# Linear attention and gated feed-forward: small PE products regrouped by array shape, accumulators moved between bank pools

## Chip, cores, metric

One core of one Trainium2 chip. The metric is the device time of one execution in microseconds (us). Of the core's engines, PE (TensorE) does the matrix products, DVE (VectorE), ACT (ScalarE) and POOL (GpSimd) the rest, and SP (SyncE) issues transfers. Matrix products are written to accumulators in PSUM, a memory that the kernel divides into banks.

## The reference, cut to what matters

```python
for b in range(nb):                                   # blocks of 64 tokens, state carried along
    intra = einsum('bhic,bhjc->bhij', qb, kb) * Dmask # scores, masked with decay
    intra = einsum('bhij,bhjd->bhid', intra, vb)
    inter = einsum('bhid,bhde->bhie', qb * lam_pow, kv_state)
    out[:, :, sl] = intra + inter
    kv_state = lam_block * kv_state + einsum('bhsd,bhse->bhde', kb_dec, vb)
# x: [3072 tokens, 512]
y = (sigmoid(x @ w_gate) * (x @ w_val)) @ w_out       # 512 -> 1536 -> 512
```

Batch 4 ("b" below), 8 heads of 64, 768 tokens. The kernel goes through the tokens in six steps of 128 (step 0 to 5). In each it makes for every b and head a score block, masks it on the DVE, multiplies it with v (masked products) and adds q times state (state products); then it renews the state (sums). The dense products of one step run between the attention work of the next.

## The kernel before

`ps_at` has five PSUM banks for attention, `ps_ff` three for the dense products.

```python
ps_at = ctx.enter_context(tc.tile_pool(name="ps_at", bufs=5, space=bass.MemoryType.PSUM))
ps_ff = ctx.enter_context(tc.tile_pool(name="ps_ff", bufs=3, space=bass.MemoryType.PSUM))
...
def piece_s(n, bs, pool=ps_at, tag="ps"):             # scores: 64 rows x 128 columns of the array
    for b in bs:
        bp, i = b // 2, b % 2
        sp = [pool.tile([128, HP, C], FP32, name=f"sp{u}", tag=tag) for u in range(2)]
        for hp in range(HP):
            for u in range(2):
                us = slice(u * 64, (u + 1) * 64)
                nc.tensor.matmul(sp[u][:, hp, :], lhsT=KS[n, bp][us, hp // 2, i, hp % 2, :],
                                 rhs=QS[n, bp][us, hp // 2, i, hp % 2, :], ...)
...
def piece_a(n, pairs):
    OP = {...ps_at.tile(...)...}
    for ...:                                          # state products: 64 x 64
        nc.tensor.matmul(OP[bp, u][half(e), x, i, :], lhsT=Sb[half(u), 2 * bp + i, 2 * e + x, :],
                         rhs=QS[n, bp][half(u), e, i, x, :], ...)
    for ...:                                          # masked products: 128 x 64
        intra(n, 2 * bp + i, OP[bp, u][:, x, i, :], 2 * x + u, False, i == 1 and x == 1)
    ...                                               # ACT copies OP into XT
...
def c(n, *pairs):                                     # sums: 128 x 64
    for bp in pairs:
        pool, tag = (ps_at, "ps") if bp == 0 or n == 0 else (ps_ff, "ff")
...
for n in range(2, NSTEP):                             # nx = n + 1
    ...
    gv(n, 10)                                         # dense: gate and value of one tile
    sc(nx, 0); gv(n, 11); m(nx, 0)                    # scores of b 0, 1; masks
    piece_po(n, 0)                                    # dense: output of one b
    sc(nx, 1); m(nx, 1)                               # scores of b 2, 3
    piece_po(n, 1); piece_po(n, 2)
    a(nx, 0, 1); c(nx, 0, 1)                          # state and masked products, sums
    piece_po(n, 3)
```

## Time and profile before

| | before |
|---|---|
| time, median of six runs | 226.31 us (226.23 to 227.33) |
| span from first to last instruction, profiled run | 224.2 us |
| PE busy | 97% of the span |
| DVE, ACT, POOL busy | 47%, 35%, 35% |
| matmuls | 1744 |

A PE row of the timeline has start, duration, line, operation, operands, the array's rows*columns, the shape, and the count of merged matmuls. The duration includes a modelled end and overlaps the next row, so read the difference of two starts. The operands are named gp (gate), vp (value) and po (output) for the dense products, sp for scores, op for state and masked products, cp for sums. An array shape of 64*128 means that two matmuls run side by side, 64*64 four, 128*64 two.

### The profile page before, as it was taken

What the parts mean: (1) busy time and instruction counts of PE and PEld (TensorE: products, weight loads), DVE (VectorE), ACT (ScalarE), POOL (GpSimd) and SP (SyncE); (2) the same over time, 40 slices, a digit from 0 to 9 for tenths busy, and PEclk for the clock granted to TensorE, in tenths of its full rate; (3) what the DMA queues carried; (4) which work ended last, traced back from release to release, by engine and by line L of the source; (5) the groups of instructions that cost most, each with busy time, mean ns of one, the idle gap of its engine ahead of it and who ended that gap; (6) DMA issues with size and microseconds to landing.
All of it is one profiled execution on the core that took longest, in us unless ns stands there. A gap on an engine that the chain in (4) does not pass through costs nothing.

```text
span 224.2 us, 4261 instructions
## 1 busy us (share of the span) xinstructions
PE 217.6 (97%) x1744; PEld 114.3 (51%) x1744; DVE 105.9 (47%) x193; ACT 79.5 (35%) x151; POOL 79.2 (35%) x78
## 2 busy tenths in 40 slices
PE   7789999999999999999999999999999999999994
PEld 2454455888854454444455444446444445444443
DVE  7797758585411713336722445642335840333300
ACT  5664343435422234333225333115333225333221
POOL 8998687983592008920006940000000000000000
PEclk9999999999999999999999999999999999999999
DMA  6999999999999993999021999021930012100022
GB/s 110 155 171 191 191 176 155 164 177 170 157 163 163 226 225 106 202 158 100 1 96 67 218 144 136 0 96 47 169 69 0 0 57 86 47 3 0 0 94 95
DMA packets 106419, 25.70 MB, mean 115 GB/s; under 512 B 97056, under 2 KB 103456, under 8 KB 106400
## 3 DMA queue, kind: packets, MB, share of 16 engines
q0 software_dynamic: 81792, 13.90, 80.4%
q1 hardware_dynamic: 23568, 11.28, 21.2%
q10 hardware_dynamic: 1040, 0.26, 0.5%
q8 instruction: 13, 0.21, 0.4%
q14 instruction: 6, 0.05, 0.1%
HBM read 28.32 MB, written 6.29 MB: 154 GB/s over the span
## 4 chain that ended last, share of the span: by engine, by line
PE 92%; DMA 3%; POOL 3%; issue 0%; ACT 0%; DVE 0%; POOLq 0%
PE po L476 27%; PE gp L413 21%; PE vp L419 20%; PE gp L427 6%; PE gp L448 5%; PE vp L454 5%; DMA vb<-in_v_dram 3%; PE op L306 3%; PE sp L293 2%; PE op L318 1%; PE po L465 1%; POOL kb L91 1%; PE cp L397 1%; POOL qb L91 1%; POOL vb L91 1%
## 5 line engine op out<-in xcount | busy, mean ns | idle before, releaser
L422 DVE TENSOR_TENSOR ht<-sg,vp 128x512 bf16<-128x512 bf16 x53 | 36.5, 688 | 62.6 <-PE vp L419 62.5
L476 PE MATMUL po<-WO,ht 128*128 128x512 bf16 x276 | 61.9, 379 | 0.0
L413 PE MATMUL gp<-XT,WG 128*128 128x512 bf16 x212 | 54.4, 379 | 0.0
L419 PE MATMUL vp<-XT,WV 128*128 128x512 bf16 x212 | 54.4, 379 | 0.0
L416 ACT ACTIVATE sg<-gp 128x512 bf16<-128x512 f32 x53 | 31.6, 597 | 59.3 <-PE gp L413 59.3
L476 PEld LDWEIGHTS <-ht 128*128 128x128 bf16 x276 | 26.3, 98 | 31.0
L419 PEld LDWEIGHTS <-WV 128*128 128x128 bf16 x212 | 20.7, 98 | 25.0
L413 PEld LDWEIGHTS <-WG 128*128 128x128 bf16 x212 | 20.4, 98 | 24.5
L479 ACT COPY ob<-po 128x512 f32<-128x512 f32 x23 | 13.5, 586 | 52.2 <-PE po L476 50.4
L204 DVE TENSOR_TENSOR MT<-sp,mask 128x512 bf16<-128x512 f32 x40 | 25.2, 683 | 8.7 <-PE sp L293 8.7
L375 POOL TENSOR_TENSOR sd<-Sb,dec 128x512 f32<-128x512 bf16 x8 | 8.2, 1042 | 40.6 <-DVE Sb L404 40.6
L448 PE MATMUL gp<-XT,WG 128*128 128x256 bf16 x96 | 14.4, 273 | 0.0
L454 PE MATMUL vp<-XT,WV 128*128 128x256 bf16 x96 | 14.4, 273 | 0.0
L458 DVE TENSOR_TENSOR ht<-sg,vp 128x256 bf16<-128x256 bf16 x24 | 10.0, 420 | 8.6 <-PE vp L454 8.6
L451 ACT ACTIVATE sg<-gp 128x256 bf16<-128x256 f32 x24 | 9.2, 384 | 13.0 <-PE gp L448 11.8
L366 POOL TENSOR_TENSOR kd<-kb,kds 128x1024 bf16<-128x1024 bf16 x6 | 11.3, 1906 | 5.0 <-DMA kb<-in_k_dram 5.0
L91 POOL DMA_DIRECT2D vb<-in_v_dram x10 | 12.7, 1279 | 0.7 <-DMA WG<-in_moe_w_gate_dram 0.6
L404 DVE TENSOR_TENSOR Sb<-cp,sd 128x512 bf16<-128x512 f32 x8 | 5.2, 686 | 15.5 <-PE cp L397 15.5
L333 ACT CAST XT<-op 128x512 bf16<-128x512 f32 x19 | 9.9, 598 | 2.1 <-PE op L306 2.0
L448 PEld LDWEIGHTS <-WG 128*128 128x128 bf16 x96 | 9.2, 98 | 1.7 <-issue 0.2
L454 PEld LDWEIGHTS <-WV 128*128 128x128 bf16 x96 | 9.4, 98 | 1.1
L77 POOL DMA_DIRECT2D qb<-in_q_dram x8 | 9.4, 1183 | 0.0
(80 smaller groups left out, 165.4 us busy)
## 6 DMA issues: line engine op xcount, KB each, us to landing
out_dram<-ob SPq DMA_DIRECT2D x21, 256.0 KB, 2.0
kb<-in_k_dram POOLq DMA_DIRECT2D x10, 256.0 KB, 8.5
qb<-in_q_dram POOLq DMA_DIRECT2D x8, 256.0 KB, 8.3
vb<-in_v_dram POOLq DMA_DIRECT2D x4, 512.0 KB, 13.9
WO<-in_moe_w_out_dram POOLq DMA_DIRECT2D x3, 512.0 KB, 8.7
WV<-in_moe_w_val_dram POOLq DMA_DIRECT2D x5, 256.0 KB, 8.7
WG<-in_moe_w_gate_dram POOLq DMA_DIRECT2D x4, 256.0 KB, 8.3
qb<-in_q_dram POOLq DMA_DIRECT2D x6, 128.0 KB, 9.0
```

The costliest lines, as they stand in the source:

```text
L91: nc.gpsimd.dma_start(out=lst[n][:, b0:b1], in_=src[b0:b1, :, sl, :].rearrange("b h s d -> s (b h) d"))
L204: nc.vector.tensor_tensor(out=out.rearrange("p (e x) c -> p e x c", e=2), in0=x.rearrange("p (e x) c -> p e x c", e=2), in1=mask.rearrange ...
L366: nc.gpsimd.tensor_tensor(out=KD[n][:, e], in0=K[n][:, e], in1=kds[:, e::2].unsqueeze(1).unsqueeze(3).to_broadcast([128, B, HP, D]), op=AL ...
L413: nc.tensor.matmul(gp, lhsT=WG[:, mt, fs], rhs=x[:, mt, :], start=(mt == 0), stop=(mt == NMT - 1))
L416: nc.scalar.activation(sg, gp, AF.Sigmoid)
L419: nc.tensor.matmul(vp, lhsT=WV[:, mt, fs], rhs=x[:, mt, :], start=(mt == 0), stop=(mt == NMT - 1))
L422: nc.vector.tensor_mul(HT[n, ft], sg, vp)
L427: nc.tensor.matmul(ps[:, lo:hi], lhsT=W[:, mt, ft * 128:(ft + 1) * 128], rhs=x[:, mt, lo:hi], start=(mt == 0), stop=(mt == NMT - 1))
L448: nc.tensor.matmul(gp[:, cs], lhsT=WG[:, mt, fs], rhs=x[:, mt, cs], start=(mt == 0), stop=(mt == NMT - 1))
L454: nc.tensor.matmul(vp[:, cs], lhsT=WV[:, mt, fs], rhs=x[:, mt, cs], start=(mt == 0), stop=(mt == NMT - 1))
L476: nc.tensor.matmul(po, lhsT=HT[n, ft][:, tt * 128:(tt + 1) * 128], rhs=WO[:, ft, :], start=(ft == 0), stop=(ft == NFT - 1))
L479: nc.scalar.copy(ob, po)
```

## The change

Its intent: fewer changes of array shape. The scores of the last b (in step 1, of every b) are cut in two halves of 64 columns, which gives them the 64x64 shape of the state products, and the state products move next to them. In steps 2 to 5 the scores of the other three b's share one visit of the PE. The second sum of each step and one dense accumulator (v11) move to the attention banks.

```diff
-    def piece_s(n, bs, pool=ps_at, tag="ps"):
+    def piece_s(n, bs, homes=("ps", "ps"), parts=1):
+        w = C // parts
...
-                    nc.tensor.matmul(sp[u][:, hp, :], lhsT=KS[n, bp][us, hp // 2, i, hp % 2, :],
+                    for z in range(parts):
+                        zs = slice(z * w, (z + 1) * w)
+                        nc.tensor.matmul(sp[u][zs, hp, :], lhsT=KS[n, bp][us, hp // 2, i, hp % 2, zs],
...
+    def piece_x(n, bp, homes=("ps", "ps")):           # the state products of the old piece_a
...
     def c(n, *pairs):
-            pool, tag = (ps_at, "ps") if bp == 0 or n == 0 else (ps_ff, "ff")
-            cp = pool.tile([128, 2, HP, D], FP32, name="cp", tag=tag)
+            cp = ps_at.tile([128, 2, HP, D], FP32, name="cp", tag="ps")
...
+    def most_scores(n):
+        piece_s(n, [0, 1])
+        piece_s(n, [2], ("ps", "ff"))
+        piece_m(n, 2, (1,))
+    def other_masks(n): ...
+    def last_scores(n):
+        piece_s(n, [3], parts=2)
+        piece_m(n, 3)
+        piece_x(n, 0)
+        piece_x(n, 1, ("ps", "ff"))
+    def rest(n):
+        piece_a(n, 0, 1)
+        if n + 1 < NSTEP:
+            c(n, 0, 1)
+    def pair(bp):                                     # step 1
+        piece_s(1, [2 * bp], ("ff", "ps"), parts=2)
+        piece_m(1, 2 * bp)
+        piece_s(1, [2 * bp + 1], parts=2)
+        piece_x(1, bp)
...
-    v11 = psum()
+    v11 = psum_at("ps").rearrange("p h c -> p (h c)")
...
-        sc(nx, 0)
+        most_scores(nx)
         gv(n, 11)
-        m(nx, 0)
+        other_masks(nx)
         piece_po(n, 0)
-        sc(nx, 1)
-        m(nx, 1)
         piece_po(n, 1)
+        last_scores(nx)
         piece_po(n, 2)
-        a(nx, 0, 1)
-        if nx + 1 < NSTEP:
-            c(nx, 0, 1)
+        rest(nx)
         piece_po(n, 3)
```

More of the change, by code (lines that the diff above doesn't have):

```diff
@@ L283, with psum_at @@
     SP = {}
-    def piece_s(n, bs, pool=ps_at, tag="ps"):
+    def psum_at(which):
+        pool, tag = (ps_ff, "ff") if which == "ff" else (ps_at, "ps")
+        return pool.tile([128, HP, C], FP32, name="sp", tag=tag)
+    def piece_s(n, bs, homes=("ps", "ps"), parts=1):
+        w = C // parts
         for b in bs:
             bp, i = b // 2, b % 2
-            sp = [pool.tile([128, HP, C], FP32, name=f"sp{u}", tag=tag) for u in range(2)]
+            sp = [psum_at(homes[u]) for u in range(2)]
             for hp in range(HP):
@@ L292, in piece_s @@
                     us = slice(u * 64, (u + 1) * 64)
-                    nc.tensor.matmul(sp[u][:, hp, :], lhsT=KS[n, bp][us, hp // 2, i, hp % 2, :],
-                                     rhs=QS[n, bp][us, hp // 2, i, hp % 2, :],
-                                     start=(hp == 0), stop=(hp == HP - 1), skip_group_check=True)
+                    for z in range(parts):
+                        zs = slice(z * w, (z + 1) * w)
+                        nc.tensor.matmul(sp[u][zs, hp, :], lhsT=KS[n, bp][us, hp // 2, i, hp % 2, zs],
+                                         rhs=QS[n, bp][us, hp // 2, i, hp % 2, :],
+                                         start=(hp == 0), stop=(hp == HP - 1), skip_group_check=True)
             SP[n, b] = sp
     def piece_m(n, b, us=(0, 1)):
-        if us[0] == 0:
+        if (n, b) not in MT:
             MT[n, b] = mtp.tile([128, 2, HP, C], BF16, tag="MT", name="MT")
@@ L308, in intra, with piece_a @@
                              start=start, stop=stop, skip_group_check=True)
-    def piece_a(n, pairs):
-        OP = {(bp, u): ps_at.tile([128, 2, 2, C], FP32, name="op", tag="ps")
-              for bp in pairs for u in range(2)}
-        for bp in pairs:
-            for i in range(2):
-                for x in range(2):
-                    for u in range(2):
-                        for e in range(2):
-                            nc.tensor.matmul(OP[bp, u][half(e), x, i, :],
-                                             lhsT=Sb[half(u), 2 * bp + i, 2 * e + x, :],
-                                             rhs=QS[n, bp][half(u), e, i, x, :],
-                                             start=(i == 0 and x == 0), stop=False,
-                                             skip_group_check=True)
+    OP = {}
+    def piece_x(n, bp, homes=("ps", "ps")):
+        for u in range(2):
+            pool, tag = (ps_ff, "ff") if homes[u] == "ff" else (ps_at, "ps")
+            OP[bp, u] = pool.tile([128, 2, 2, C], FP32, name="op", tag=tag)
+        for i in range(2):
+            for x in range(2):
+                for u in range(2):
+                    for e in range(2):
+                        nc.tensor.matmul(OP[bp, u][half(e), x, i, :],
+                                         lhsT=Sb[half(u), 2 * bp + i, 2 * e + x, :],
+                                         rhs=QS[n, bp][half(u), e, i, x, :],
+                                         start=(i == 0 and x == 0), stop=False,
+                                         skip_group_check=True)
+    def piece_a(n, *pairs):
         for bp in pairs:
@@ L332, in piece_a @@
                 cp = nc.vector.tensor_copy if n == 1 and bp == 0 and u else nc.scalar.copy
-                cp(XT[n][:, u::2, 2 * bp:2 * bp + 2, :], OP[bp, u])
+                cp(XT[n][:, u::2, 2 * bp:2 * bp + 2, :], OP.pop((bp, u)))
     def piece_a0(b, split=()):
@@ L511, in first @@
     def first():
-        piece_s(0, [2], ps_ff, "ff")
+        piece_s(0, [2], ("ff", "ff"))
         piece_m(0, 2, (0,))
@@ L544, in t, with other_masks @@
         piece_t(n, bp)
-    def sc(n, bp):
-        piece_s(n, [2 * bp, 2 * bp + 1])
-        piece_m(n, 2 * bp)
-    def m(n, bp):
-        piece_m(n, 2 * bp + 1)
-    def a(n, *pairs):
-        piece_a(n, pairs)
+    def most_scores(n):
+        piece_s(n, [0, 1])
+        piece_s(n, [2], ("ps", "ff"))
+        piece_m(n, 2, (1,))
+    def other_masks(n):
+        piece_m(n, 0)
+        piece_m(n, 1)
+        piece_m(n, 2, (0,))
+    def last_scores(n):
[12 more added lines that the diff above has]
+        piece_x(1, bp)
     def gv(n, *fts):
@@ L607 @@
     prod(0, 9, v9)
-    sc(1, 0)
-    m(1, 0)
+    pair(0)
+    piece_m(1, 1)
     gv(0, 10)
@@ L613 @@
     sigm(0, 11, g11)
-    a(1, 0)
-    v11 = psum()
+    piece_a(1, 0)
+    v11 = psum_at("ps").rearrange("p h c -> p (h c)")
     mm_part(v11, WV, 0, 11, 0, TCH)
@@ L623 @@
     gvh(1, 0, 6, 7)
-    sc(1, 1)
+    pair(1)
     gvh(1, 0, 8)
-    m(1, 1)
+    piece_m(1, 3)
     gvh(1, 0, 9, 10)
-    a(1, 1)
+    piece_a(1, 1)
     c(1, 0, 1)
@@ L640 @@
     piece_po(0, 3)
-    sc(2, 0)
-    m(2, 0)
+    most_scores(2)
+    other_masks(2)
     piece_po(1, 0)
-    sc(2, 1)
-    m(2, 1)
     piece_po(1, 1)
+    last_scores(2)
     piece_po(1, 2)
-    a(2, 0, 1)
-    c(2, 0, 1)
+    rest(2)
     piece_po(1, 3)
```

## The prediction

> **What bounds the kernel now.** I read the page's head first, then who waited for whom on the PE, then the PE in order of time, then the DVE and the DMA landings at the places where the PE is late.
>
> ```profile
> span 224.2 us, 4261 instructions
> PE 217.6 (97%) x1744; PEld 114.3 (51%) x1744; DVE 105.9 (47%) x193; ACT 79.5 (35%) x151; POOL 79.2 (35%) x78
> PE wm L153 <- DVE ip L119: 1.2, 1, 1.2
> PE tk L238 <- DMA kb<-in_k_dram: 0.5, 1, 0.5
> ```
>
> The PE is busy for 97% of the span at a granted clock of 1.000, every other engine for at most half, and the longest waits of the matmuls lie in the first microseconds. So the time is the PE's stream, and a change that leaves its matrix work alone can only win what stands between the matmuls. The busy column hides that: a matmul of 512 columns is given 379 ns, though in a run they start 216 ns apart. I therefore count from start to start. One step of the loop, PE in order of time (start us, us, engine line, operation, names, array rows*columns, shape, count):
>
> ```profile
> 104.91 1.03 PE L419 MATMUL vp<-XT,WV 128*128 128x512 bf16 x4
> 105.87 0.62 PE L293 MATMUL sp<-QS,KR 64*128 64x128 bf16 x16
> 106.42 1.04 PE L413 MATMUL gp<-XT,WG 128*128 128x512 bf16 x4
> ...
> 108.16 2.75 PE L476 MATMUL po<-WO,ht 128*128 128x512 bf16 x12
> 110.85 0.62 PE L293 MATMUL sp<-QS,KR 64*128 64x128 bf16 x16
> 111.40 5.35 PE L476 MATMUL po<-WO,ht 128*128 128x512 bf16 x24
> 116.68 0.64 PE L318 MATMUL op<-QS,Sb 64*64 64x128 bf16 x32
> 117.25 1.08 PE L306 MATMUL op<-MT,vb 128*64 128x128 bf16 x32
> 118.17 0.67 PE L397 MATMUL cp<-vb,kd 128*64 128x64 bf16 x32
> 118.78 2.76 PE L476 MATMUL po<-WO,ht 128*128 128x512 bf16 x12
> ```
>
> What to see: the four vp matmuls take 105.87 - 104.91 = 0.96 us, where four others take 0.86 (4 x 216 ns). The missing 0.10 us is spent whenever the array shape (the number pair) changes next. It is there again at 110.85 (2.69 for twelve, against 12 x 0.216 = 2.59), at 116.68 (5.28 against 5.18), after each group of scores, from 64*64 to 128*64, and from 128*64 back to 128*128. It is not there between op and cp at 118.17, which share 128*64: 0.92 for 16 pairs of 56 ns. The single records give the rest: in 64*128 two score matmuls start 3 to 4 ns apart and the next pair 56 ns after the last; in 64*64 four matmuls start 3 to 4 ns apart and the next four 56 ns later; the first step of a group adds 10 to 24 ns. So 16 scores are 8 x 56 + 10 + 0.10 us = 0.55, as shown, and 32 state products are 8 x 56 + 24 + 0.10 us = 0.57, as shown.
>
> **What the Trainium skill says.** "TensorEngine Tiling (Array Packing)", Key Properties: changing the tiling mode, not just the tile, drains the TensorE. The trace agrees: 0.10 us at each change of shape and none without. "TensorE: Matmul & The Clock Gate", Part 3: tiles of one mode run at the same time, about 4 ns apart; the trace has 3 to 4 ns. "Perfetto Trace Analysis", TensorE lifecycle: the reported end of a matmul is an estimate; the trace agrees (379 against 216 ns). The same page, Optimizing Tensor Performance: independent groups should rotate through PSUM banks so that evacuation overlaps the next group; two places below show what a short rotation costs here.
>
> **The change, part by part.**
> Changes of shape. In each of steps 2 to 5 the PE now leaves the dense products three times: for scores (in, out), for scores (in, out), and for state products, masked products and sums (in, 64*64 to 128*64, out). That is 7 changes. The new order on the PE, read from both built programs, is 24 scores in 64*128 (in, out), then after two output groups 16 half-width scores and 32 state products all in 64*64 (in, out), then after one more output group masked products and sums in 128*64 (in, out): 6 changes. Step 1 has for each of its two pairs of b 2 + 3 = 5 changes and gets 2 + 2 = 4, as both its score groups become 64*64 and stand with the state products. So 4 + 2 = 6 changes go, plus a few ns of group start: 6 x 0.105 = 0.63 us.
>
> Added matmuls. The halved scores make 8 extra matmuls and 8 extra weight loads for each b so treated: one in each of steps 2 to 5, four in step 1, so 64 in all (1744 becomes 1808). A b had 8 score matmuls in 4 pairs and gets 16 in 4 fours; a pair in 64*128 and a four in 64*64 both take 56 ns, so 4 x 56 = 224 ns before and after. So I put the cost at zero.
>
> Banks. Accumulators rotate: the dense products through three banks, attention through five, so a new one waits for the reader of the third (fifth) back. Two waits of the PE are of this kind, too short for the wait view because the estimated ends cover them (two PE lines, then the DVE line that ends the wait):
>
> ```profile
> 39.51 0.60 PE L454 MATMUL vp<-XT,WV 128*128 128x256 bf16 x4
> 40.08 0.60 PE L448 MATMUL gp<-XT,WG 128*128 128x256 bf16 x4
> 39.34 0.69 DVE L440 TENSOR_TENSOR ht<-sg,gp 128x512 bf16<-128x512 bf16 x1 [0.34 <-PE gp L427]
> ...
> 51.44 0.60 PE L454 MATMUL vp<-XT,WV 128*128 128x256 bf16 x4
> 52.07 0.60 PE L448 MATMUL gp<-XT,WG 128*128 128x256 bf16 x4
> 50.91 1.29 DVE L404 TENSOR_TENSOR Sb<-cp,sd 128x512 bf16<-128x512 f32 x2 [0.64 <-PE cp L397]
> ```
>
> Four 256-column matmuls take 0.437 us elsewhere. From 39.51 they take 0.57: the next gp wants the bank of v11, free at 39.34 + 0.69 = 40.03, and starts at 40.08, 0.14 late. From 51.44 they take 0.63: vp wants the third bank back, that of the second sum, which the DVE leaves at 50.91 + 1.29 = 52.20. This costs 0.20. In the new kernel v11 and that sum take attention banks; the third one back is then one that the ACT has read long before. Both waits should go: 0.34 us. In steps 2 to 4 the same kind of sum costs nothing today (the output group after it hides it).
>
> Sum: 0.63 + 0.34 = 0.97 us, all on the PE's path, out of 226.27: 225.3 us. The start-up (to 34 us) and the last step's dense work are untouched.
>
> **The rivals.**
> 1. New bank waits. Scores of three b's hold all five attention banks and one dense bank. A mask takes 0.60 us from start to start on the DVE. In step 3 the 24 scores would end near 106.8; the mask that frees the dense bank ends near 107.5, and its next user, an output group, starts near 108.4. The other five masks follow the last gate product (near 109.3) and end near 112.3; the first small matmul that needs one of their banks is at 113.7. So margins are 0.9 and 1.3 us. In step 1 they are thin: the masked products of the first pair would start near 37.5 with the last mask done near 37.3, and those of the second pair need the last mask about 0.3 us after it is done. A wait here would give back 0.1 to 0.3 us: 225.6.
> 2. The issue of small matmuls becomes the bound. 48 in a row in 64*64 at 14 ns each, instead of 32 (or 16 in step 1), with weight loads of 106 ns against 94 for the 64*128 ones. For: no run of this length is in the trace. Against: 32 + 32 + 32 small ones stand in a row at 116.68 with no slowing, the last 32 still at 16 ns each. If the halves cost double, 8 x 0.22 us would be lost: near 227.1.
> 3. A transfer takes the place of the wait. The first transposed K of step 2 lands at 72.14, and the scores start at 73.00; they would now come near 73.00 - 0.21 - 0.34 = 72.45. That leaves 0.3 us. Earlier output stores share the queues; if the landing slips, up to 0.3 us comes back. Later landings (95.4 for use at 105.9) are far away.
> 4. Nothing at all for the bank waits, if the DVE's queue is simply as late for the next user: the new owner of each bank is one read by the ACT or earlier by the DVE, so I think it unlikely; it would make 225.6.
>
> **Range and chances.** The 0.63 is counted from six repeats of one size and is firm; the 0.34 may lose some to rivals 1 or 3, so the high end is 226.0. Below, nothing else is on offer: 224.8 allows for run-to-run spread (the three runs before span 226.23 to 227.33). The 2% line is 4.5 us; no part comes near it on the fast side, and only rival 2 doubled again would on the slow side. Faster 0.005, same 0.985, slower 0.01.
>
> **What would show it.** Changes of shape: six PE groups of 64*64 scores followed at once by state products 56 ns later per four, the output group before the masked products ending 0.10 us late, 6 changes per step; the period of steps 3 to 5, 34.6 us from one step's first scores to the next (105.87 to 140.47), shrinks by 0.10. Added matmuls: 1808 on the PE, a 16-matmul half-width group in 0.22 us; 0.45 would be rival 2. Banks: every run of four 256-column matmuls in step 1 in 0.44 us except before a change of shape. Transfer: step 2's first scores directly after the output group, not at a landing. The prediction is wrong if the span falls by less than 0.4 us or more than 1.5.

## The result and the profile after

| | before | after |
|---|---|---|
| time, median of six runs | 226.31 us | 225.06 us (224.93 to 225.54) |
| ratio | | 0.9944, 95% interval 0.9926 to 0.9963 |
| span, profiled run | 224.2 us | 223.2 us |
| time less span, profiled run | 2.12 us | 1.77 us |

A ratio here is the mean time of one kernel's runs over that of the other's in the same rounds, so not quite the ratio of the medians. The interval lies clear of 1: the kernel is 0.4 to 0.7% faster.

The head of the page after:

```profile
span 223.2 us, 4384 instructions
PE 216.4 (97%) x1808; PEld 114.0 (51%) x1808; DVE 106.6 (48%) x193; ACT 79.0 (35%) x151; POOL 79.2 (36%) x78
```

The PE has its 64 extra matmuls and is still the bound. The timeline of the PE after, for the step that the prediction shows:

```profile
104.22 1.03 PE L428 MATMUL vp<-XT,WV 128*128 128x512 bf16 x4
105.18 0.84 PE L299 MATMUL sp<-QS,KR 64*128 64x128 bf16 x24
105.96 1.04 PE L422 MATMUL gp<-XT,WG 128*128 128x512 bf16 x4
...
107.69 5.34 PE L485 MATMUL po<-WO,ht 128*128 128x512 bf16 x24
112.97 0.42 PE L299 MATMUL sp<-QS,KR 64*64 64x128 bf16 x16
113.21 0.62 PE L326 MATMUL op<-QS,Sb 64*64 64x128 bf16 x32
113.76 2.76 PE L485 MATMUL po<-WO,ht 128*128 128x512 bf16 x12
116.46 1.08 PE L312 MATMUL op<-MT,vb 128*64 128x128 bf16 x32
117.37 0.67 PE L406 MATMUL cp<-vb,kd 128*64 128x64 bf16 x32
```

The halved scores start at 112.97 and the state products 0.24 us later: 4 x 56 ns and the start of the group, with no time for a change of shape between. One b's scores and the state products together take 0.79 us (112.97 to 113.76). The shape now changes six times. The next step's first scores start at 139.67 in the single records, 34.49 us after 105.18; before it was 34.60.

In step 1, the stretches that the prediction names as bank waits, in the PE's timeline after:

```profile
39.36 0.60 PE L463 MATMUL vp<-XT,WV 128*128 128x256 bf16 x4
39.80 0.60 PE L457 MATMUL gp<-XT,WG 128*128 128x256 bf16 x4
...
51.05 0.60 PE L463 MATMUL vp<-XT,WV 128*128 128x256 bf16 x4
51.48 0.60 PE L457 MATMUL gp<-XT,WG 128*128 128x256 bf16 x4
```

Both are 0.44 and 0.43 us from start to start now, against 0.57 and 0.63 before.

Where the time went, between the two profiled runs (226.31 and 224.93 us, 1.38 apart): from the last dense group before step 1's first scores (33.075 before, 33.034 after) to the last group of the last output (220.498, 219.487) the PE needs 187.423 and 186.453 us, 0.97 less. The start-up is 0.04 shorter, the tail 0.02. The other 0.35 us lie outside the span (2.12 against 1.77 us of time less span); the prediction had no term for them. Below, "the stretch" is this one of 187.423 and 186.453 us.

### The profile page after: what moved, and what is told of

Its sections match the earlier page's. It is cut to its first block, busy times and chain, and to the rows that moved or that the text cites. A ratio compares the mean times of both kernels' runs of the same rounds, so it can differ in the third digit from the quotient of the medians.

```text
span 223.2 us, 4384 instructions
## 1 busy us (share of the span) xinstructions
PE 216.4 (97%) x1808; PEld 114.0 (51%) x1808; DVE 106.6 (48%) x193; ACT 79.0 (35%) x151; POOL 79.2 (36%) x78
## 4 chain that ended last, share of the span: by engine, by line
PE 92%; DMA 3%; POOL 3%; issue 0%; ACT 0%; DVE 0%; POOLq 0%
PE po L485 27%; PE gp L422 21%; PE vp L428 21%; PE gp L436 5%; PE gp L457 5%; PE vp L463 5%; DMA vb<-in_v_dram 3%; PE op L312 3%; PE sp L299 3%; PE po L474 1%; POOL kb L91 1%; PE cp L406 1%; PE op L326 1%; POOL qb L91 1%; POOL vb L91 1%; PE sp L436 0%
```

## The experiments

All times are medians; before is 226.35 to 226.38 us on the chips of the experiments, and after is 225.06 us (224.93 to 225.54) from its own run. A difference to after is thus one between runs of different rounds; the ratios are to before, from the same rounds. Where a cause hangs on a few tenths of a us, the stretch of the PE in the traces decides.

**1. The banks alone, in the kernel before.**

```diff
-            pool, tag = (ps_at, "ps") if bp == 0 or n == 0 else (ps_ff, "ff")
-            cp = pool.tile([128, 2, HP, D], FP32, name="cp", tag=tag)
+            cp = ps_at.tile([128, 2, HP, D], FP32, name="cp", tag="ps")
-    v11 = psum()
+    v11 = ps_at.tile([128, TCH], FP32, name="gp", tag="ps")
```

> The kernel before, with only v11 and the second sum of each step moved to attention banks; order and array shapes untouched. My theory (two bank waits of 0.14 and 0.20 us in step 1, nothing in steps 2 to 4): 0.34 us less than before on the PE's path, about 225.95 us; in the trace the stretches of four 256-column matmuls after v11 and after the sums of step 1 take 0.44 us instead of 0.57 and 0.63. Rival (the banks do nothing, all the gain is from the shape changes): within 0.05 us of before. Rival (the banks are most of the gain): near 225.1.

Measured: 226.01 us (225.95 to 226.90; ratio to before 0.9987, interval 0.9971 to 1.0004). The PE needs 187.093 us for the stretch that took 187.423: 0.33 less. The interval of the times touches 1, so the verdict rests on the trace: both delays are gone. In the PE's timeline of this run:

```profile
39.51 0.60 PE L453 MATMUL vp<-XT,WV 128*128 128x256 bf16 x4
39.95 0.60 PE L447 MATMUL gp<-XT,WG 128*128 128x256 bf16 x4
...
51.30 0.60 PE L453 MATMUL vp<-XT,WV 128*128 128x256 bf16 x4
51.74 0.60 PE L447 MATMUL gp<-XT,WG 128*128 128x256 bf16 x4
```

The banks are a gain of their own, a third of what the PE won.

**2. The banks undone, in the kernel after.**

```diff
-            cp = ps_at.tile([128, 2, HP, D], FP32, name="cp", tag="ps")
+            pool, tag = (ps_at, "ps") if bp == 0 or n == 0 else (ps_ff, "ff")
+            cp = pool.tile([128, 2, HP, D], FP32, name="cp", tag=tag)
-    v11 = psum_at("ps").rearrange("p h c -> p (h c)")
+    v11 = psum()
```

> The kernel after, with v11 and the second sum of each step back in the dense products' banks. If the banks are a separate gain: 0.34 us more than after, about 225.4. But I now count the rotation in the new order: in steps 2 to 4 the last output group would then take the bank of a state product that the ACT copies out only about 1.05 us after that group could start, so I expect 3 x 1.05 + 0.34 = 3.5 us more than after, about 228.5, slower than before: the banks are then not an extra gain but what makes the new order possible.

Measured: 225.40 us (225.15 to 225.46; 0.9953, 0.9939 to 0.9967), 0.34 more than after. The PE's timeline of this run has the second delay back:

```profile
51.25 0.60 PE L464 MATMUL vp<-XT,WV 128*128 128x256 bf16 x4
51.89 0.60 PE L458 MATMUL gp<-XT,WG 128*128 128x256 bf16 x4
```

That is 0.64 us for four matmuls. The first delay is back too (39.43 to 40.00 in the single records), and the stretch is 186.787 us, 0.33 over after. So experiments 1 and 2 split the PE's 0.97 us alike: 0.33 for the banks, 0.64 for the rest of the change. The first part of what I expected held, the second fell: no output group waits in steps 2 to 4 (the last one of step 3 starts at 118.38, right behind the sums, while the ACT copies state products out until 119.51). I had assumed that banks are handed out in strict rotation. The built program, which names the bank of every accumulator, says that they are not: in step 3 this output group gets the bank of the output group before it, and the state product's bank goes to the gate product behind it.

**3. The new order with whole scores.** `parts=2` dropped at its three places.

```diff
-        piece_s(n, [3], parts=2)
+        piece_s(n, [3])
```

> The kernel after in its order, but the scores beside the state products in whole 64x128 form: one more change of shape in each of steps 2 to 5 and one for each of the two pairs of step 1, 6 in all, and 64 matmuls fewer (1744). My theory: 6 x 0.105 = 0.63 us more than after, about 225.7. Rival (halving costs PE time that eats part of the gain): less than 0.4 us more, or even faster. Rival (the order, not the shape, gives the gain): same as after within 0.1.

Measured: 225.64 us (225.53 to 225.78; 0.9967, 0.9951 to 0.9983), 0.58 more than after. The PE's timeline of this run:

```profile
113.21 0.40 PE L299 MATMUL sp<-QS,KR 64*128 64x128 bf16 x8
113.53 0.64 PE L326 MATMUL op<-QS,Sb 64*64 64x128 bf16 x32
114.11 2.76 PE L485 MATMUL po<-WO,ht 128*128 128x512 bf16 x12
```

Eight whole scores take 0.32 us up to the state products, where sixteen halves take 0.24: half the instructions, but 0.08 us more, because the shape changes behind them. The state products, now the start of a group, take 0.02 us more as well. The PE's stretch is 187.090 us, 0.64 over after. It is also that of experiment 1 (187.093), which has the same banks in the old order with the old shapes: the new order by itself wins nothing.

**4. Halved scores, state products moved back.**

```diff
     def last_scores(n):
         piece_s(n, [3], parts=2)
         piece_m(n, 3)
-        piece_x(n, 0)
-        piece_x(n, 1, ("ps", "ff"))
     def rest(n):
+        piece_x(n, 0)
+        piece_x(n, 1, ("ps", "ff"))
         piece_a(n, 0, 1)
```

and likewise for the pairs of step 1.

> The kernel after with halved scores, but the state products back beside the masked products: again 7 changes of shape in a step and 5 for a pair, 1808 matmuls. My theory: 0.63 us more than after, about 225.7, the same as the unsplit version to 0.1 us. Rival (what helps is that the scores are halved, or that three b's share a visit): within 0.1 us of after.

Measured: 225.77 us (225.63 to 226.20; 0.9973, 0.9958 to 0.9989), 0.71 more than after; the PE's stretch is 187.203 us, 0.75 more. The timeline shows the change at 113.35 paid on its own, and another between 116.39 and 116.96:

```profile
113.35 0.42 PE L299 MATMUL sp<-QS,KR 64*64 64x128 bf16 x16
113.70 2.76 PE L485 MATMUL po<-WO,ht 128*128 128x512 bf16 x12
116.39 0.64 PE L326 MATMUL op<-QS,Sb 64*64 64x128 bf16 x32
116.96 1.08 PE L312 MATMUL op<-MT,vb 128*64 128x128 bf16 x32
```

It is 0.11 us over experiment 3, 0.02 in each of six places: in the single records the halved scores alone take 0.350 us and the whole ones 0.327, mostly because the first step of a 64x64 group costs 24 ns and that of a 64x128 group 10. Halving without moving, or moving without halving, wins nothing over the stretch of experiment 1; the pair of them does.

**5. All scores of steps 2 to 5 halved.**

```diff
-        piece_s(n, [0, 1])
-        piece_s(n, [2], ("ps", "ff"))
+        piece_s(n, [0, 1], parts=2)
+        piece_s(n, [2], ("ps", "ff"), parts=2)
```

> The kernel after, with the scores of the first three b's halved too, so that in steps 2 to 5 all scores run in 64x64: 96 matmuls and 96 weight loads more (1904), no change of shape more or less. My theory (a pair in 64x128 and a four in 64x64 both take 56 ns): the visit of three b's goes from 0.776 to 0.79 us (a longer first group), 0.06 us more in all, about 225.1. Rival (issue or weight loads bind when 48 small matmuls follow each other): the visit takes 1.0 us or more, at least 1 us more in all, above 226.

Measured: 225.15 us (225.06 to 225.66; 0.9944, 0.9931 to 0.9957). In the single records the visit of three b's takes 0.796 us against 0.776. So 96 more matmuls and weight loads in runs of 48 cost what their first step costs; issue does not bind. The profiled run was the slowest of the five (225.66 us), and its trace shows why: the wait view and the PE's timeline have

```profile
PE sp L299 <- DMA KR<-kb: 0.6, 1, 0.6
...
73.05 0.86 PE L299 MATMUL sp<-QS,KR 64*64 64x128 bf16 x48 [0.56 <-DMA KR<-kb]
```

The scores of step 2 stood ready and waited for their transposed k, which landed at 73.01. This is the prediction's third rival, seen in one execution.

**6. Two needless changes of shape.** Only the second of the three b's is halved.

```diff
-        piece_s(n, [0, 1])
+        piece_s(n, [0])
+        piece_s(n, [1], parts=2)
```

> The kernel after, with only the second of the first three b's halved: the visit goes 64x128, 64x64, 64x128, two changes of shape more in each of steps 2 to 5, 8 in all, and nothing else on the path. My theory (0.105 us for a change with its group start): 8 x 0.105 = 0.84, up to 8 x 0.12 = 0.96 us more than after, about 226.0. Rival (what costs is leaving and entering the dense 128x128 form, a change between two small forms is cheap): less than 0.3 us more.

Measured: 225.89 us (225.77 to 225.97; 0.9977, 0.9965 to 0.9989), 0.83 more than after. In the PE's timeline the visit

```profile
105.33 1.07 PE L299 MATMUL sp<-QS,KR 64*128 64x128 bf16 x32
106.33 1.04 PE L422 MATMUL gp<-XT,WG 128*128 128x512 bf16 x4
```

takes 1.00 us instead of 0.78 (105.18 to 105.96); the row merges both shapes under the first one's name. From the single records it is 0.230 us for two changes, group starts included, in each of four steps. A change between two small shapes costs as much as one to or from the dense shape.

**7. One visit fewer: the second sum of step 0 moved into a visit of its own shape.**

```diff
-    c(0, 1)
-    keep(1)
...
     piece_a(1, 0)
+    c(0, 1)
...
     prod(0, 11, v11)
+    keep(1)
```

and the decay of that half on GpSimd moved behind the loads of q and k of step 2.

> The kernel after, and the second sum of step 0 (128x64), which has a visit of its own between dense products, moved behind the masked products of the first pair of step 1 (128x64 too); its decay on GpSimd moves behind the loads of q and k of step 2. Two changes of shape fewer. My theory: 0.2 us less than after, about 224.85. Rival (the moved decay or load order makes the scores of step 2 wait for their transposed k, or the sum's reader is late): same as after or slower, with a gap before the scores of step 2.

Measured: 225.52 us (225.07 to 226.16; 0.9964, 0.9952 to 0.9976), 0.46 more than after. The theory of 0.2 us less fell, and so did the first part of the rival: no wait stands before the scores of step 2. The 0.46 us are all in the stretch (186.899 us, 0.45 over after). In step 1 the sum now costs 0.25 us in the open: masked products and sum take 0.471 + 0.350 us, the masked products alone 0.570. And a bank wait of 0.20 us is back, in the PE's timeline of this run:

```profile
40.83 0.60 PE L463 MATMUL vp<-XT,WV 128*128 128x256 bf16 x4
41.46 0.60 PE L457 MATMUL gp<-XT,WG 128*128 128x256 bf16 x4
```

In the built program this gp has the bank of the gp two groups before it, in after that of the vp three before. So moving the sum and its reader changed the hand-out of banks.

Nothing was won in the start-up for it. In the trace after, the weight that the PE needs behind the removed visit lands at 18.92 and is used at 19.10, so less than 0.2 of the 0.47 us that the visit took could be saved. In the timeline of this run

```profile
16.87 1.03 PE L436 MATMUL gp<-XT,WG 128*128 128x512 bf16 x4
18.66 1.04 PE L436 MATMUL gp<-XT,WV 128*128 128x512 bf16 x4 [0.77 <-DMA WV<-in_moe_w_val_dram]
```

the PE even waits for an earlier weight, which lands at 18.61 where every other trace has it at 16.98 to 17.44. This run took 225.72 us; whether the move delays that weight or only this execution did is open. Two changes of shape fewer won nothing where the next weight was hardly there.

**8. Five tiny DVE writes, in a new tile.** This and the next two ask about the time outside the span.

```diff
+    pad = const.tile([128, 1], FP32, tag="pad")
+    for _ in range(5):
+        nc.vector.memset(pad, 0.0)
     piece_po(0, 0)
```

> The kernel after, with five tiny writes of the DVE added where it is idle, so that it has as many instructions as in the kernel before (312 against 307). This asks where the part of the gain comes from that lies outside the span: time less span is 2.11 to 2.18 us in every run of the kernel before and of the banks-only version, 1.73 to 1.84 in all others, and of what I can count only the DVE's instructions sort them so. If the count decides: span as after (223.2 to 223.3), time less span 2.1 to 2.2, so about 225.4. If not: time less span 1.8, about 225.06.

Measured: 227.47 us (227.28 to 227.88; 1.0050, 1.0038 to 1.0062). The count of DVE records is 310, not 312 (some separate waits went), time less span is 1.97 to 2.02. But the span rose to 225.6: the start-up is 0.73 us longer, and the PE waits 1.6 us for the transposed k of step 2, which lands at 74.75. The run does not answer cleanly; it needed the next two.

**9. The kernel before with fewer DVE instructions** (the decay table of step 1 on is filled with ones). Its output is wrong, which doesn't matter for the time.

```diff
-    lamq_start()
+    nc.vector.memset(lp, 1.0)
-    lamq_double(1, 2, 4, 8)
-    lamq_double(16, 32, 64)
```

> The kernel before with its nine small DVE instructions that build the decay table replaced by one write (wrong on purpose from step 1 on), all on an engine that idles there. It asks the question of the time outside the span from the other side. If the DVE's instruction count decides (312 gives 2.15, 307 and 306 give 1.78): span as before (224.0 to 224.3), time less span about 1.8, so about 226.0. If not: time less span 2.15, about 226.35.

Measured: 225.84 us (225.83 to 226.06; 0.9981, 0.9967 to 0.9994); the span stays (224.0 to 224.3 in five runs), time less span is 1.74 to 1.83, where the nine runs of before beside it have 2.09 to 2.18. The count of DVE records is 304.

**10. Seven tiny DVE writes in the kernel after, into a tile that exists.**

```diff
+    for _ in range(7):
+        nc.vector.memset(loc[:, 0:1], 0.0)
     piece_po(0, 0)
```

> The kernel after with seven tiny DVE writes at the same idle place as in the run with five, but into a tile that exists already, so that no address moves. If the five writes' slow run came from the new 4-byte tile, which moved the tiles behind it (its first transposed k landed at 74.75 instead of 71.99): the span is back at 223.2 to 223.7. If from the writes themselves: 225 or more. If the DVE's count decides the time outside the span: time less span 2.0 to 2.2 (five writes gave 1.97 to 2.02 with 310 instructions); if not, 1.8.

Measured: 225.38 us (225.28 to 225.91; 0.9962, 0.9949 to 0.9974). The count is 312; the profiled span is 223.2, as after, and time less span 2.08 to 2.18. So with 304, 306 or 307 DVE records in the trace (the page's 193 leaves out separate waits and others that are not counted as busy) the time outside the span is 1.78 us on average, with 310 it is 1.99, with 312 it is 2.13 to 2.15, in both kernels and whatever the PE's count is (1744 matmuls in experiment 3, 1904 in experiment 5: both 1.79). The kernel before has 312, of which 116 are separate waits; after has 307, with 111. That is the missing 0.35 us. That the count moves this time is shown; what happens in it is not, as it lies before the first or behind the last traced instruction. It also shows that the writes were not what slowed run 8; its new tile is the other difference. In the built program that tile moves the q, k and v tiles behind it by 32 bytes per partition, off multiples of 256. The first load into a moved tile (k, issued at 1.26 in both) lands at 7.99 instead of 7.32, one into an unmoved tile (q0f) at 4.96, as in after (4.95). That the new addresses are the cause fits, but no run moved them alone.

**11. The transposed k earlier.** From the waits in runs 5 and 8: the loads of v of step 2 and of q, k, v of step 3 are held back until the first transposed k has landed.

```diff
-    load(2, "qkv", 0, B)
+    load(2, "qk", 0, B)
...
     make_kd(2)
+    nc.gpsimd.tensor_copy(loc[:, 0:1], KS[2, 0][:, 0, 0, 0, 0:1])
+    load(2, "v", 0, B)
     load(3, "qkv", 0, B)
```

> The kernel after, with the loads of v of step 2 and of q, k and v of step 3 held back until the first transposed k has landed (a tiny GpSimd copy that reads it stands before them). The transposes of step 2 then have the DMA to themselves: I expect the transposed k at 64 to 69 instead of 72 to 73, against scores at 72.4, and with it no run in which the PE waits there: median 225.0, lowest as after (224.9), the spread of 224.9 to 225.5 narrower. If the late landing was not what spread the runs of after: same median and spread. If v or the loads of step 3 now come late: slower, with a DMA wait at the masked products of step 2 or the scores of step 3.

Measured: 225.02 us (224.90 to 225.04; 0.9940, 0.9928 to 0.9953), correct. In its timelines of SP (issue of the transpose) and POOL (the copy that reads it):

```profile
60.17 1.51 SPq L229 DMA_TRANSPOSE KR<-kb  x1
...
65.63 0.18 POOL L659 CAST loc<-KR 128x1 f32<-128x1 bf16 x1 [3.40 <-DMA KR<-kb]
```

The transposed k is there at 65.6 instead of 72.0, 6.9 us before the scores at 72.5, and the five runs lie within 0.14 us, where those of after lie within 0.61 us. This is the lowest median, 0.04 us under after, with a narrower spread. That the slow runs of after waited for this transfer is not shown: only run 5's and run 8's traces have such a wait.

## Why the prediction was right or wrong

Point by point, by its own steps:

- **The bound.** Right: the PE's stream lost 0.97 us, the predicted sum to the hundredth.
- **Changes of shape, 0.63 us.** Right. Undone in two ways they cost 0.64 and 0.75 us of PE time (runs 3 and 4), and eight needless changes cost 0.92 (run 6). Run 3 also rules out that the order alone did it.
- **Added matmuls, zero.** Right, also for 96 more of them (run 5).
- **Banks, 0.34 us.** Right in size (0.33 alone, 0.34 in the time of run 2), wrong in the reading of the second wait. The prediction has the vp at 51.44 wait for the DVE's sum, free at 52.20. But the late one is the gp behind it, and it starts at 52.07, before that. In ACT's timeline of the kernel before stands

```profile
51.63 0.38 ACT L451 ACTIVATE sg<-gp 128x256 bf16<-128x256 f32 x1 [0.19 <-PE gp L448]
```

which ends at 52.01. The matmul at 52.07 waits, by its record, for the ACT's semaphore alone, and in the built program it has the bank of the gp two groups before it, the one that this ACT row reads. So banks do not rotate strictly, as the prediction has it; with one of three held by the sum, two are left for the dense products next to it. The cure worked under either reading, as it takes the sum off the dense banks. The release must come before the start; that check would have shown the error.
- **Rival 1, new bank waits.** Did not come: the masked products of step 1 start without delay.
- **Rival 2, issue.** Did not come.
- **Rival 3, the transfer.** It did not come in the profiled run of after, but it was underrated. The 72.14 us of the prediction is the first of sixteen completion signals of that transpose; the last is at 72.56. Read so, scores at 72.45 would have had to wait. They did not, because the landing came earlier too: 71.99 against scores at 72.42, a margin of 0.43 us, where before it is 0.44. In the traces, runs 8 and 11 aside, the landing lies between 71.9 and 73.0. So this transfer is close to a second bound before the change and after it; in run 5 it is one, and run 11 takes it away.
- **Rival 4, no gain from the banks.** Did not come: run 1 wins 0.33 us on the PE.
- **The sum, 0.97 us, 225.3 us.** Short by 0.24 us against the median. The missing term is the time outside the span, 0.35 us with the five DVE waits that the new order drops. Nothing in the trace of before pointed to it; only time less span over many kernels did. The range held it, but by its allowance for spread, not because the term was foreseen.

## What to carry to other kernels

On a PE-bound kernel, count changes of array shape on the PE's own order and read starts, not busy time: 0.10 us each here, and splitting a product so that it joins its neighbour's shape was free. Ask before moving a piece of work whether the PE is the bound where it stands; in the start-up it hardly was, and the move of run 7 won nothing there and cost 0.45 us in step 1. When the busiest engine gets faster, look for the transfer that is just in time, and check each named releaser against the clock: it must end before the start it explains.

## What the Trainium skill lacked or had wrong

- "TensorEngine Tiling (Array Packing)", Key Properties, says that a change of mode drains the TensorE, without a size: 0.09 to 0.10 us here, between every two shapes met here, and 10 ns (64x128) to 24 ns (64x64) more for the first step of a group.
- "TensorE: Matmul & The Clock Gate", Back-to-back issue gap, gives about 131 ns per matmul of 512 columns and 81 ns for 128 columns in a stream of weight loads and matmuls. Here, with one weight load for each matmul, it is 216 ns and, for transposes of 128 columns, 56 ns, which are the section's own figures for a matmul by itself; a pair in 64x128 or a four in 64x64 also takes 56 ns.
- No page that I read says that the DVE's instruction count moves the time outside the first and last traced instruction: 1.78 us with up to 307 DVE records, 1.99 with 310, 2.13 to 2.15 with 312.
